# Second-layer sums of a dense network cut 16, 16 and 10 products long, beside an attention that shares TensorE

## Chip, cores and metric

The kernel runs on one core of one Trainium2 chip. The metric is device time in microseconds (us) of one execution, the median of several runs; less is better. The granted TensorE clock reads full speed through the whole profiled execution.

## What is computed

The input x has 2048 rows of 512. It is normalised by row, and the normalised rows go two ways: through an attention with 32 heads of width 16 that all share one key and one value projection, and through a dense network with 1792 hidden values. The result is x plus the product of the two.

```python
x = A_x
xn = _layernorm(x, axis=-1)
s = _A_ref(xn, A_wq, A_wk, A_wv, A_wo)          # attention
g = _silu(_B_ref(xn, B_w1, B_b1, B_w2))         # dense network
return x + s * g

def _A_ref(x, wq, wk, wv, wo):
    q = (x @ wq).reshape(B, S, H, Dh).transpose(0, 2, 1, 3)
    k = x @ wk
    v = x @ wv
    scores = jnp.einsum("bhqd,bkd->bhqk", q, k) * (Dh ** -0.5)
    p = _softmax(scores, axis=-1)
    o = jnp.einsum("bhqk,bkd->bhqd", p, v)
    return o.transpose(0, 2, 1, 3).reshape(B, S, H * Dh) @ wo

def _B_ref(x, w1, b1, w2):
    h = jnp.einsum("bsd,df->bsf", x, w1) + b1
    sp = jnp.log1p(jnp.exp(-jnp.abs(h))) + jnp.where(h > 0, h, 0)
    act = h * jnp.tanh(sp)                       # Mish
    return jnp.einsum("bsf,fd->bsd", act, w2)
```

## The kernel before

**Numbers.** Matrix products are made from float32 values split into a high and a low part. A product of two such values is three matmuls (`TERMS`, L56: high by high, high by low, low by high). Each of these is called a dense product below when it belongs to a projection or to the network.

**Attention in 512 steps.** The 2048 rows are cut into four chunks of 512 columns, and the work into 512 steps, sixteen for each of the 32 pairs of chunk and group of four heads. A step has

- four score products, `e` in the profile (L1056, function `score`), each over 64 rows of the array, then an exponent of each on ScalarE (ACT), `pts<-e` (L1061);
- four products for the largest score of a row, `m` (L1084, function `m_one`), also over 64 rows, each followed on VectorE (DVE) by a maximum, `mb<-m` (L1088). They run 22 steps ahead (`LEAD`);
- four value products, `pv` (L1142), over all 128 rows, from exponents made two steps earlier.

**Two halves of the array.** A 64-row product uses one half of TensorE's rows, and two of them, one on each half, run side by side. They are called a pair here. A dense product of 128 rows is split into its upper and its lower 64 rows (`Mm.half`, L114), and these dense halves, `xps` in the profile, fill the half of the array that the scores leave free. In one step the dense halves lie on one side and the scores on the other; in the next step the sides are exchanged.

**Buffers.** PSUM has three buffers for `e`, three for `m`, one for the dense sum and one for `pv`. The fourth `e` in a row therefore takes the buffer of the first one and needs its exponent done, and the fourth `m` needs the maximum of the first.

**Dense groups.** The dense work is a queue of groups, each a sum in one PSUM buffer: the query projections, the first layer (function `m1_group`), the output projections (`wo_groups`) with 12 products each, and the second layer. The second layer's 14 weight tiles give 42 products for each of 16 row tiles. They are cut into three parts (`THIRDS`, L53: tiles 0 to 4, 5 to 9, 10 to 13; function `m2_groups`), so 15, 15 and 12 products, whose sums are added by ACT and DVE outside PSUM.

**How a group is laid over steps.** There are two ways.

- Function `waves` (L610) lays a group of 12 over four steps of 6 halves: a step takes 6 dense products' halves on one side, the next step their other halves. With 6 halves one `m` goes to the dense side too, so that a step is seven pairs.
- Function `unit` (L672) lays a whole group over a block of four steps. A block has two halves; in each, the dense halves go through in a row on one side, while eight `e` and the `m` of two steps stand on the other, in the order of the string `UNIT` (L48). In it, E is a score product, M a max product, x stands for a place with a dense half alone, and 0 for a place with an `m` on the dense side and an `e` on the other. The last m takes a buffer of the scores. Behind the places stand two steps' `pv`. A block is used where a group of more than 12 and at most 15 products is ready at a step that four divides (`unit_ready`, L1541); a longer group that is not ready then goes through `waves`.

The Python code that writes the instructions decides all of this before the kernel runs. It keeps its own estimates of the time of a step (`K_US`, `UNIT_US`) to decide when transfers are issued and which group is ready.

**Weights.** Second-layer and output weights go through a ring of five tiles on the chip (`wbs`, L203); a group waits in the queue until its tiles are there. The query projection is copied by ACT into a tile `qf` (L741), split by GpSimd (POOL) into `qh` and `ql`, and moved by DMA into the query tiles `qt`. The attention's last step adds x, held in one of four tiles `xr`.

Of the kernel before, what the change touches and what calls it, by code (L numbers as in the profile page):

```python
# [41 lines left out]
STEP_US = 2.88  # L42
K_US = {-1: 2.3, 0: 2.7, 6: 2.86, 7: 3.07, 8: 3.07}
UNIT_US = 11.75
XMAX = 8
NPT = 14
EM = "MEMEMEME"
UNIT = "0MEMExEMEMEMEMEm"  # L48
MLAG = 4
NHB = 4  # L50
NACT = 10
AHEAD = 5
THIRDS = ((0, 5), (5, 10), (10, 14))  # L53
TMAX = 2.0 ** 14
EMAX = 2.0 ** 60
# [67 lines left out]
def block_kernel(ctx: ExitStack, tc: tile.TileContext, x, wq, wk, wv, wo, w1, b1, w2, out):  # L123
# [78 lines left out]
    b1c = cp.tile([P, NFT], F32, name="b1c")  # L202
    wbs = cp.tile([P, 5, 2, D], F32R, name="wbs")  # L203
    pts = cp.tile([P, NPT, C], F32, name="pts")
# [163 lines left out]
    def v_copy(c):  # L368
        vt_of[c] = sb.tile([P, C], F32, tag="xr", name=f"vt{c}", bufs=4)
# [26 lines left out]
    load_x(0)  # L396
    wkv = sb.tile([P, C], F32, tag="xr", name="wkv", bufs=4)
    wkv = wkv[:, 0:2 * NDT * DH].rearrange("p (a t n) -> p a t n", a=2, t=NDT)
# [41 lines left out]

    RING = {"wq": 1, "ws": 2, "wb": 5, "wx": 4}
    NRAW = {"wq": 1, "ws": 1, "wb": 1, "wx": 1}
# [23 lines left out]
    def home(tag, k):  # L466
        if tag == "wx":
            return (xt_of[NC] if k else new_xt(NC))[:, :, k]
        if tag == "ws" and k < 12 and k % 6 < 4:
            return xt_of["w"][:, :, k % 6]  # L470
        if tag == "wb":
            return wbs[:, (k - 1) % 5]
        return sb.tile([P, 2, D], F32R, tag=tag, name=f"{tag}{k}", bufs=RING[tag])

# [35 lines left out]
    def load(tag):  # L510
# [6 lines left out]
        it = its[n]  # L517
        if taken(tag, n) and (tag != "ws" or kept.get(it.key)):
            return
        if n == k and kept.get(it.key):  # L520
# [86 lines left out]
    def chunk_size(n):  # L607
        return -(-n // -(-n // XMAX)) if n else 0

    def waves(h, em, new):  # L610
# [44 lines left out]
        if k and not done:  # L655
# [5 lines left out]
            else:  # L661
                cur["chunk"] = mms

    def mm12(lhs, rhs, n, late=False):
        res = []
        tot = 3 * n
        for j, a, b in ([(j, a, b) for a, b in ((0, 0), (0, 1), (1, 0)) for j in range(n)] if late else
                        [(j, a, b) for j in range(n) for a, b in TERMS]):
            res.append(Mm(pe, lambda j=j, a=a: lhs(j, a), lambda j=j, b=b: rhs(j, b), len(res), tot))
        return res  # L670

    def unit(s, h):  # L672
# [24 lines left out]
        for n, op in enumerate(UNIT):  # L697
            if n == 8:
                due(t + 0.5)
                pump()  # L700
                due(t + 1)
            if op == "0":
                m_one(h)
                op = "E"
            elif xs:
                x_one()
# [23 lines left out]
    def q_group(c, b):  # L730
        it = item("wq", ("q", b), wq[:, P * b:P * (b + 1)].rearrange("(t p) n -> p t n", p=P))

        def post(ps):
# [3 lines left out]
            if first:  # L737
                act.activation(qh, ps, AF.Copy)
                lead["q"](lambda: sub(dve, ql, ps, f(qh)))
            else:  # L740
                qf = sb.tile([P, C], F32, tag="qf", name=f"qf{c}_{b}", bufs=1)  # L741
                act.activation(qf, ps, AF.Copy)
                gap[0] += 1
                hi_pool(qh, qf)
                sub(pool, ql, qf, f(qh))
            for k in range(2):
# [20 lines left out]
    t_hist = [-10 ** 6] * 2  # L767
    xr_hist = [-10 ** 6] * 4
    hb_hist = [-10 ** 6] * NHB
# [79 lines left out]

    def m2_groups(c, third, its, m1s):  # L850
        lo, hi = THIRDS[third]

        def ready(tt):
            done = m1_done.get((c, hi - 1))
            return None if done is None else done - g_of[tt].most
# [3 lines left out]
        def mk(tt):  # L859
            def post(ps):  # L860
# [36 lines left out]
                def s3():  # L897
# [22 lines left out]
    def wo_groups(c):  # L920
# [4 lines left out]
        def mk(tt):  # L925
# [79 lines left out]

    def w2_items(c, k):
        lo, hi = THIRDS[k]
        return [item(("wb", "wx")[(c, k) == (NC - 1, 2)], ("2", ft), w2[P * ft:P * (ft + 1), :]) for ft in range(lo, hi)]

# [9 lines left out]
    for c in range(NC):  # L1019
        for k in range(3):  # L1020
# [5 lines left out]
            take(THIRDS[k][1] - THIRDS[k][0] - 2)  # L1026
            g2 = m2_groups(c, k, w2_items(c, k), None)
            if (c, k) == (NC - 1, 1):
# [164 lines left out]
    def turn_rows():  # L1193
        t = sb.tile([P, C], F32, tag="qf", name="turns", bufs=1)
        for e in range(2):
# [345 lines left out]
    def unit_ready(s):  # L1541
# [151 lines left out]
```

## Time and profile before

| | |
|---|---|
| median of 3 runs | 1564.72 us (1564.71 to 1564.95) |
| span of the profiled execution | 1564.5 us; the profile gives no other time of it, and the median lies 0.2 us above |
| TensorE matmuls | 11715, busy 99% of the span |
| TensorE weight loads | 56% |
| VectorE | 86% |
| ScalarE | 83% |
| GpSimd | 41% |
| 16 DMA engines | 25%, 125 MB |
| attention steps with 6 dense halves | 362 |
| blocks of four steps | 31 |
| other steps with 8 or 7 dense halves | 2 and 2 |
| last steps, after the last max product | 22 |

The counts of steps and blocks are those of the program's order on TensorE. In the profile a line of a group has the engine, the operation, the tile written and those read, the count, the busy time, the mean time of one in ns, and the idle time of the engine before it with what ended it. In the time line a row has its start, its length (of several merged instructions: from the first start to the last end), the engine, the line of the code, the operation and its tiles. PEld is TensorE's load of weights, which can run beside a matmul.

A matmul's time in the time line overlaps with that of the next one on the same rows of the array. What counts is the distance from start to start.

### The profile page before, as it was taken

Reading aid. Unit: us, or ns where it says so; the run is one execution under the profiler, and the core shown is the slowest. Engines: PE = TensorE matmul, PEld = TensorE weight load, DVE = VectorE, ACT = ScalarE, POOL = GpSimd, SP = SyncE. Lnnn points to the kernel's source line nnn. Section 1 sums busy time; section 2 is a strip of 40 time slices with the busy share of each in tenths; the row PEclk is TensorE's granted clock in tenths of the full one; section 3 lists DMA queues with packets and bytes.
Section 4 is the critical chain, followed back from the end, with each engine's and each line's share of the span. In section 5 each row is a group of like instructions: output and inputs, shape, how many; then the busy total and the mean of one; then the engine's idle time right before and its main releaser. Section 6 shows DMA issues by size and latency. Waiting matters only on the chain.

```text
span 1564.5 us, 31399 instructions
## 1 busy us (share of the span) xinstructions
PE 1553.6 (99%) x11715; PEld 877.1 (56%) x11715; DVE 1347.6 (86%) x2279; ACT 1292.8 (83%) x2509; POOL 635.1 (41%) x667
## 2 busy tenths in 40 slices
PE   9999999999999999999999999999999999999998
PEld 6555655655555565565555556556555555655644
DVE  7998888888989988888898988888889998888844
ACT  6588888789888778977989787897788978888796
POOL 4787449365356203331615422163152323314122
PEclk9999999999999999999999999999999999999999
DMA  6333134133141303212113220322321213031110
GB/s 197 106 132 118 46 104 146 29 112 112 51 153 50 107 16 112 72 27 98 51 59 109 92 92 18 103 67 78 104 59 45 93 57 112 23 98 32 29 67 28
DMA packets 72083, 125.47 MB, mean 80 GB/s; under 512 B 19742, under 2 KB 33356, under 8 KB 71932
## 3 DMA queue, kind: packets, MB, share of 16 engines
q1 hardware_dynamic: 71500, 122.68, 24.8%
q8 instruction: 93, 1.52, 0.4%
q10 hardware_dynamic: 432, 0.79, 0.1%
q14 instruction: 58, 0.48, 0.1%
HBM read 75.57 MB, written 26.21 MB: 65 GB/s over the span
## 4 chain that ended last, share of the span: by engine, by line
PE 97%; DVE 2%; ACT 1%; POOL 0%; issue 0%; DVEq 0%
PE xps L116 43%; PE pv L1142 32%; PE m L1084 12%; PE e L1056 7%; DVE mb L1088 1%; PE xps L112 1%; PE warm L1310 1%; PE kp L350 0%; PE xp L309 0%; PE wop L116 0%; ACT pts L1061 0%; DVE e L888 0%; PE y2ps L116 0%; PE wop L112 0%; ACT hb L800 0%; ACT xt L318 0%
## 5 line engine op out<-in xcount | busy, mean ns | idle before, releaser
L1088 DVE TENSOR_REDUCE mb<-m 128x1 f32<-128x512 f32 x2048 | 1266.4, 683 | 167.5 <-PE m L1084 104.7
L1061 ACT ACTIVATE pts<-e 128x512 f32<-128x512 f32 x2048 | 1066.1, 607 | 219.9 <-PE e L1056 157.1
L1084 PE MATMUL m<-ks,qt 48*128 48x512 f32 (+1 forms) x2048 | 844.1, 425 | 1.3 <-DVE mb L1088 1.3
L1056 PE MATMUL e<-qt,ks 64*128 64x512 f32 x2048 | 748.8, 407 | 0.0
L1142 PE MATMUL pv<-pts,vaug 128*32 128x512 f32 x4096 | 532.9, 603 | 0.0
L1084 PEld LDWEIGHTS m<-ks,qt 48*128 48x128 f32 (+1 forms) x2048 | 369.9, 185 | 105.8 <-DVE mb L1088 50.8
L1056 PEld LDWEIGHTS e<-qt,ks 64*128 64x128 f32 x2048 | 373.5, 186 | 27.3 <-ACT pts L1061 22.8
L116 PE MATMUL xps<-wbs,act 64*128 64x512 f32 x1248 | 314.4, 397 | 0.0
L116 PE MATMUL xps<-xt,ws 64*128 64x512 f32 x1128 | 312.3, 410 | 1.7 <-ACT pts L1061 0.9
L116 PEld LDWEIGHTS xps<-xt,ws 64*128 64x128 f32 x1128 | 194.8, 185 | 185.6 <-ACT pts L1061 122.3
L116 PEld LDWEIGHTS xps<-wbs,act 64*128 64x128 f32 x1248 | 226.5, 185 | 64.8 <-ACT pts L1061 32.7
L1142 PEld LDWEIGHTS pv<-pts,vaug 128*32 128x32 f32 x4096 | 87.6, 108 | 150.6 <-issue 141.9
L169 POOL TENSOR_TENSOR hb<-hb,t 128x512 f32<-128x512 f32 x56 | 72.1, 1287 | 162.4 <-ACT t L819 82.1
L179 POOL TENSOR_SCALAR t<-t 128x512 f32<-128x512 f32 x56 | 34.4, 615 | 184.0 <-ACT t L806 183.9
L116 PE MATMUL xps<-xt,wq 64*128 64x512 f32 x336 | 93.0, 410 | 0.0
L116 PEld LDWEIGHTS xps<-xt,wq 64*128 64x128 f32 x336 | 58.0, 185 | 55.0 <-ACT pts L1061 37.7
L169 POOL TENSOR_TENSOR oc<-oc,sc 128x512 f32<-128x512 f32 (+1 forms) x16 | 20.6, 1289 | 153.4 <-DMA wbs<-w 71.2
L116 PE MATMUL xps<-wbs,ot_all 64*128 64x512 f32 x288 | 79.3, 408 | 0.0
L116 PEld LDWEIGHTS xps<-wbs,ot_all 64*128 64x128 f32 x288 | 49.6, 185 | 46.8 <-ACT pts L1061 28.5
L169 POOL TENSOR_TENSOR act<-hb,act 128x512 fp32r<-128x512 f32 x56 | 72.1, 1288 | 4.7
L169 POOL TENSOR_TENSOR hb<-hb,u 128x512 f32<-128x512 f32 x56 | 72.1, 1288 | 4.4
L169 POOL TENSOR_TENSOR u<-u,t 128x512 f32<-128x512 f32 x56 | 72.0, 1285 | 4.7
(160 smaller groups left out, 885.5 us busy)
## 6 DMA issues: line engine op xcount, KB each, us to landing
wbs<-w SPq DMA_DIRECT2D x38, 512.0 KB
ws<-w SPq DMA_DIRECT2D x36, 512.0 KB
qt<-qh SPq DMA_DIRECT2D x256, 32.0 KB
w<-wbs SPq DMA_DIRECT2D x14, 512.0 KB
wq<-wq SPq DMA_DIRECT2D x14, 512.0 KB
wbs<-wo SPq DMA_DIRECT2D x12, 512.0 KB
rawws<-in_dram SPq DMA_DIRECT2D x20, 256.0 KB
w<-ws SPq DMA_DIRECT2D x10, 512.0 KB
```

Source lines behind the costliest of these rows:

```text
L112: self.pe.matmul(ps, self.lhs(), self.rhs(), start=(self.k == 0), stop=(self.k == self.tot - 1))
L116: i = self.pe.matmul(ps, self.lhs()[o], self.rhs()[o], start=(self.k == 0 and self.halves == 0), stop=(self.k == self.tot - 1 and self.hal ...
L169: eng.tensor_tensor(out=o, in0=a, in1=b, op=op)
L179: pool.tensor_scalar(o, o, lim, 0.0, op0=ALU.min, op1=ALU.max)
L1056: pe.matmul(e, ks[o:o + 64, P * k:P * (k + 1)], q[o:o + 64, p], start=True, stop=True)
L1061: x = act.activation(dst, e, AF.Exp, scale=0.25)
L1084: pe.matmul(m, q[o, p, P * t:P * (t + 1)], ks[o, C * kb:C * (kb + 1)], start=True, stop=True)
L1088: return dve.reduce_max(out=mb_of[v][:, kb, z:z + 1], in_=m, axis=AX.X)
L1142: pe.matmul(o[32 * j:32 * j + 32], vaug[:, k], pt, start=(k == 0), stop=(k == 15))
L1310: pe.matmul(warm, qts[0][:, 0, 0:P], qts[0][:, 0], start=True, stop=True)
```

## The change

The second layer's 42 products of a row tile stand in one list, weight tile by weight tile, and are cut at 16 and 32: parts of 16, 16 and 10 products for 15, 15 and 12. A cut can now fall within a weight tile, so tiles 5 and 10 are used by two parts. The items for weights are made once for each chunk and tile (`w2_item`), not once for each part.

The string `UNIT` becomes sixteen places that all have a dense half on one side and an `e` or an `m` on the other: the `m` that stood beside the first `e` moves to the place that had a dense half alone. Blocks take groups of up to 16.

A group of 10 is laid over two steps of 6 and two of 4 halves (`chunk_size` rounds up to an even number).

The ring of second-layer weights gets a sixth tile. Room for it comes from `qf`, which goes (ACT copies into `ql` itself, and POOL subtracts in place), and from the fourth `xr` tile; the last row tile's x goes to an `hb` tile. Two of the planner's estimates, for steps with 0 and with 4 halves, are new.

```diff
-K_US = {-1: 2.3, 0: 2.7, 6: 2.86, 7: 3.07, 8: 3.07}
+K_US = {-1: 2.3, 0: 2.65, 4: 2.68, 6: 2.86, 7: 3.07, 8: 3.07}
-UNIT = "0MEMExEMEMEMEMEm"
+UNIT = "EMEMEMEMEMEMEMEm"
+CUTS = (0, 16, 32, 42)
+NWB = 6
...
-    wbs = cp.tile([P, 5, 2, D], F32R, name="wbs")
+    wbs = cp.tile([P, NWB, 2, D], F32R, name="wbs")
...
-    RING = {"wq": 1, "ws": 2, "wb": 5, "wx": 4}
+    RING = {"wq": 1, "ws": 2, "wb": NWB, "wx": 4}
...
+        if tag == "wb" and n == NWB - 1 and todo["ws"][0] < 10:
+            return
...
     def chunk_size(n):
-        return -(-n // -(-n // XMAX)) if n else 0
+        m = -(-n // -(-n // XMAX)) if n else 0
+        return m + m % 2
...
+    def mm_list(lhs, rhs, terms):
+        return [Mm(pe, lambda j=j, a=a: lhs(j, a), lambda j=j, b=b: rhs(j, b), n, len(terms))
+                for n, (j, a, b) in enumerate(terms)]
...
     def unit(s, h):
-            if op == "0":
-                m_one(h)
-                op = "E"
-            elif xs:
+            if xs:
                 x_one()
...
-                qf = sb.tile([P, C], F32, tag="qf", name=f"qf{c}_{b}", bufs=1)
-                act.activation(qf, ps, AF.Copy)
+                act.activation(f(ql), ps, AF.Copy)
                 gap[0] += 1
-                hi_pool(qh, qf)
-                sub(pool, ql, qf, f(qh))
+                hi_pool(qh, f(ql))
+                sub(pool, ql, f(ql), f(qh))
...
-    xr_hist = [-10 ** 6] * 4
+    xr_hist = [-10 ** 6] * 3
...
-    def m2_groups(c, third, its, m1s):
+    w2_terms = [(j, a, b) for j in range(NFT) for a, b in TERMS]
+
+    def m2_groups(c, third):
         lo, hi = THIRDS[third]
+        terms = w2_terms[CUTS[third]:CUTS[third + 1]]
+        fts = sorted({j for j, a, b in terms})
+        its = [w2_item(c, j) for j in fts]
...
-            g = Group(mm12(lambda j, a: act_of[c, lo + j][:, a, P * tt:P * (tt + 1)],
-                           lambda j, b: its[j].tile[:, b], hi - lo), post, its, [lambda: ready(tt)])
+            g = Group(mm_list(lambda j, a: act_of[c, j][:, a, P * tt:P * (tt + 1)],
+                              lambda j, b: w2_of[c, j].tile[:, b], terms), post, its, [lambda: ready(tt)])
...
-            g.late = 3 if hi - lo == 5 else 2
+            g.late = len(its) - 2
...
-                if xr_hist[-4] is None:
-                    return False
-                st["x"] = sb.tile([P, D], F32, tag="xr", name=f"xr{t}", bufs=4)
-                st["free"] = hold(xr_hist)
+                if last and tt == 3:
+                    st["x"] = sb.tile([P, D], F32, tag="hb", name=f"xr{t}", bufs=NHB)
+                    st["free"] = lambda: None
+                else:
+                    if xr_hist[-3] is None:
+                        return False
+                    st["x"] = sb.tile([P, D], F32, tag="xr", name=f"xr{t}", bufs=3)
+                    st["free"] = hold(xr_hist)
...
-        return ok and 12 < len(cur["g"].mms) <= len(UNIT) - 1
+        return ok and 12 < len(cur["g"].mms) <= len(UNIT)
```

Two places on TensorE carry the prediction. In the rows `e_k_p_a` is a score product on side a (0 or 1), `m_a_n` a max product on side a, `xps` a dense half. The change adds lines above, so its line numbers are 2 to 14 higher. The first place is the start of the first half of the block at step 68, before and with the change; the dense halves are on side 0.

```order
1216 L1084 MATMUL m_0_20_3867<-ks,qt_79 128x512
1217 L1056 MATMUL e_4_0_1_3870<-qt_78,ks 128x512
1218 L116 MATMUL xps<-wbs,act_5_1624 128x512
1219 L1084 MATMUL m_1_20_3874<-ks,qt_79 128x512
1220 L116 MATMUL xps<-wbs,act_5_1624 128x512
1221 L1056 MATMUL e_4_1_1_3878<-qt_78,ks 128x512
1222 L116 MATMUL xps<-wbs,act_5_1624 128x512
1223 L1084 MATMUL m_1_21_3882<-ks,qt_79 128x512
1224 L116 MATMUL xps<-wbs,act_6_1718 128x512
1225 L1056 MATMUL e_5_0_1_3886<-qt_78,ks 128x512
1226 L116 MATMUL xps<-wbs,act_6_1718 128x512 x2
1227 L1056 MATMUL e_5_1_1_3891<-qt_78,ks 128x512
```

The same place with the change:

```order
1236 L118 MATMUL xps<-wbs,act_5_1625 128x512
1237 L1070 MATMUL e_4_0_1_3881<-qt_78,ks 128x512
1238 L118 MATMUL xps<-wbs,act_5_1625 128x512
1239 L1098 MATMUL m_1_20_3885<-ks,qt_79 128x512
1240 L118 MATMUL xps<-wbs,act_6_1716 128x512
1241 L1070 MATMUL e_4_1_1_3889<-qt_78,ks 128x512
1242 L118 MATMUL xps<-wbs,act_6_1716 128x512
1243 L1098 MATMUL m_1_21_3893<-ks,qt_79 128x512
1244 L118 MATMUL xps<-wbs,act_6_1716 128x512
1245 L1070 MATMUL e_5_0_1_3897<-qt_78,ks 128x512
1246 L118 MATMUL xps<-wbs,act_7_1935 128x512
1247 L1098 MATMUL m_1_22_3901<-ks,qt_79 128x512
```

The half's first max product stood in the first place, on the dense side (row 1216); now its first is in the second place, on the side of the scores (row 1239), and a dense half stands in the first. Where two dense halves came in a row (row 1226) a max product now stands between them (row 1247). All eight `m` of a half are on the side of the scores.

The second place is step 102, the third step of a group of the third part, before and with the change, up to the value products (of the repeated dense halves some rows are left out).

```order
1685 L116 MATMUL xps<-wbs,act_12_3675 128x512
1686 L1084 MATMUL m_1_24_5263<-ks,qt_78 128x512
1687 L116 MATMUL xps<-wbs,act_12_3675 128x512
1688 L1056 MATMUL e_6_0_1_5267<-qt_77,ks 128x512
1690 L1084 MATMUL m_1_25_5271<-ks,qt_78 128x512
1692 L1056 MATMUL e_6_1_1_5275<-qt_77,ks 128x512
1694 L1084 MATMUL m_1_26_5279<-ks,qt_78 128x512
1696 L1056 MATMUL e_7_0_1_5283<-qt_77,ks 128x512
1697 L1084 MATMUL m_0_24_5286<-ks,qt_78 128x512
1698 L1056 MATMUL e_7_1_1_5289<-qt_77,ks 128x512
```

The same place with the change:

```order
1718 L1098 MATMUL m_1_24_5281<-ks,qt_78 128x512
1719 L118 MATMUL xps<-wbs,act_13_3864 128x512
1720 L1070 MATMUL e_6_0_1_5285<-qt_77,ks 128x512
1721 L118 MATMUL xps<-wbs,act_13_3864 128x512
1722 L1098 MATMUL m_1_25_5289<-ks,qt_78 128x512
1723 L118 MATMUL xps<-wbs,act_13_3864 128x512
1724 L1070 MATMUL e_6_1_1_5293<-qt_77,ks 128x512
1725 L1098 MATMUL m_0_24_5296<-ks,qt_78 128x512
1726 L1070 MATMUL e_7_0_1_5299<-qt_77,ks 128x512
1727 L1098 MATMUL m_0_25_5302<-ks,qt_78 128x512
1728 L1070 MATMUL e_7_1_1_5305<-qt_77,ks 128x512
```

Seven pairs became six: two dense halves are gone, and a second `m` went to the dense side. The first score stays in the second pair, and the fourth score moves from the seventh pair to the sixth.

The order of the dense groups, the 140 steps at which one begins, the number of blocks (31) and the order of ACT's instructions are the same before and with the change. Of the steps with 6 halves, 26 become steps with 4. One second-layer group that goes through `waves`, at steps 160 to 163, had 8, 8, 7 and 7 halves and has 8 in each step. Three third parts lie in the last 22 steps.

More of the change, by code (lines that the diff above doesn't have):

```diff
@@ L368, in v_copy @@
     def v_copy(c):
-        vt_of[c] = sb.tile([P, C], F32, tag="xr", name=f"vt{c}", bufs=4)
+        vt_of[c] = sb.tile([P, C], F32, tag="xr", name=f"vt{c}", bufs=3)
         if c == 0:
@@ L396, in block_kernel @@
     load_x(0)
-    wkv = sb.tile([P, C], F32, tag="xr", name="wkv", bufs=4)
+    wkv = sb.tile([P, C], F32, tag="xr", name="wkv", bufs=3)
     wkv = wkv[:, 0:2 * NDT * DH].rearrange("p (a t n) -> p a t n", a=2, t=NDT)
@@ L471, in home @@
         if tag == "wb":
-            return wbs[:, (k - 1) % 5]
+            return wbs[:, (k - 1) % NWB]
         return sb.tile([P, 2, D], F32R, tag=tag, name=f"{tag}{k}", bufs=RING[tag])
@@ L662, in waves @@
                 cur["chunk"] = mms
+    def mm_list(lhs, rhs, terms):
+        return [Mm(pe, lambda j=j, a=a: lhs(j, a), lambda j=j, b=b: rhs(j, b), n, len(terms))
+                for n, (j, a, b) in enumerate(terms)]
     def mm12(lhs, rhs, n, late=False):
[L665 to L670, printed above, removed]
+        return mm_list(lhs, rhs, [(j, a, b) for a, b in TERMS for j in range(n)] if late else
+                       [(j, a, b) for j in range(n) for a, b in TERMS])
     def unit(s, h):
@@ L848, in m1_group @@
         return g
-    def m2_groups(c, third, its, m1s):
+    w2_terms = [(j, a, b) for j in range(NFT) for a, b in TERMS]
+    def m2_groups(c, third):
         lo, hi = THIRDS[third]
+        terms = w2_terms[CUTS[third]:CUTS[third + 1]]
+        fts = sorted({j for j, a, b in terms})
+        its = [w2_item(c, j) for j in fts]
         def ready(tt):
-            done = m1_done.get((c, hi - 1))
+            done = m1_done.get((c, fts[-1]))
             return None if done is None else done - g_of[tt].most
@@ L1004, in xt_loads, with w2_item @@
         g.start = lambda: (old(), loads())
-    def w2_items(c, k):
-        lo, hi = THIRDS[k]
-        return [item(("wb", "wx")[(c, k) == (NC - 1, 2)], ("2", ft), w2[P * ft:P * (ft + 1), :]) for ft in range(lo, hi)]
+    w2_of = {}
+    def w2_item(c, ft):
+        if (c, ft) not in w2_of:
+            tag = "wx" if c == NC - 1 and ft > THIRDS[2][0] else "wb"
+            w2_of[c, ft] = item(tag, ("2", ft), w2[P * ft:P * (ft + 1), :])
+        return w2_of[c, ft]
     qqueue.extend(q_group(c, b) for c in range(NC) for b in range(4))
@@ L1026, in block_kernel @@
             take(THIRDS[k][1] - THIRDS[k][0] - 2)
-            g2 = m2_groups(c, k, w2_items(c, k), None)
+            g2 = m2_groups(c, k)
             if (c, k) == (NC - 1, 1):
@@ L1193, in turn_rows @@
     def turn_rows():
-        t = sb.tile([P, C], F32, tag="qf", name="turns", bufs=1)
+        t = sb.tile([P, C], F32, tag="ql", name="turns", bufs=1)
         for e in range(2):
```

## Prediction, made before the change was run

> **What bounds the kernel now.** I read the page first: the shares of the engines and the chain that ended last.
>
> ```profile
> PE 1553.6 (99%) x11715; PEld 877.1 (56%) x11715; DVE 1347.6 (86%) x2279; ACT 1292.8 (83%) x2509; POOL 635.1 (41%) x667
> PE 97%; DVE 2%; ACT 1%; POOL 0%; issue 0%; DVEq 0%
> ```
>
> TensorE is busy 99% of the span and the chain runs through it for 97%. That reads as "fewer products, less time". But a matmul that was let in late is busy too, so the share doesn't say whether the array streams or waits. The time line of single steps does. Next I read busy times by stretch: the block shown below, the sum over all 31, then 80 steps of 6 halves in a row.
>
> ```profile
> 184.03:195.91 11.88, 11.88 (x98) 7.74 (x94) 9.62 (x17) 10.00 (x19) 5.11 (x5) 1.00 0.23 59
> ...
> sum 372.09, PE 372.09 PEld 238.72 DVE 320.93 ACT 296.52 POOL 110.82; mean PE 12.00 PEld 7.70 DVE 10.35 ACT 9.57 POOL 3.57
> 312.68:541.38 228.70, 228.70 (x1764) 123.57 (x1756) 205.88 (x349) 197.54 (x380) 115.79 (x117) 1.00 0.30 94
> ```
>
> A block takes 12.00 us on average, 11.88 where nothing disturbs it; a step of 6 halves takes 228.70 / 80 = 2.86. The change touches the 31 blocks and 26 of the steps. So two questions decide: what ends a block's half, and what ends a step.
>
> **A block's half.** This is the time line from 184.03 on, the first half of the block at step 36. The rows are its two first max products, the maxima, the exponents, and the end.
>
> ```profile
> 185.00 0.50 PE L1084 MATMUL m<-ks,qt 48*128 48x512 f32 x1
> 185.34 0.40 PE L116 MATMUL xps<-wbs,act 64*128 64x512 f32 x1
> 185.34 0.39 PE L1084 MATMUL m<-ks,qt 48*128 48x512 f32 x1
> 185.53 4.28 DVE L1088 TENSOR_REDUCE mb<-m 128x1 f32<-128x512 f32 x7 [1.20 <-PE e L1056]
> 185.56 3.04 ACT L1061 ACTIVATE pts<-e 128x512 f32<-128x512 f32 x6 [0.25 <-PE e L1056]
> ...
> 188.07 0.18 PEld L1084 LDWEIGHTS m<-ks,qt 48*128 48x128 f32 x1
> 188.07 0.50 PE L1084 MATMUL m<-ks,qt 48*128 48x512 f32 x1
> ...
> 188.41 0.39 PE L1056 MATMUL e<-qt,ks 64*128 64x512 f32 x1
> 188.59 0.39 PE L116 MATMUL xps<-wbs,act 64*128 64x512 f32 x1
> 188.66 0.18 PEld L1084 LDWEIGHTS m<-ks,qt 48*128 48x128 f32 x1
> 188.66 0.50 PE L1084 MATMUL m<-ks,qt 48*128 48x512 f32 x1
> 189.09 0.64 PE L1142 MATMUL pv<-pts,vaug 128*32 128x512 f32 x4
> ```
>
> The dense halves run from 185.34 to 188.59 in fourteen distances, 0.23 us each: that is the time of a pair. The maxima run without a pause from 0.03 us after the first m has ended. Seven take 4.28 us, so they follow each other in (4.28 - 0.68) / 6 = 0.60 us, slower than the max products come, one in two pairs or 0.46 us. The seventh m needs the fourth maximum's buffer. That maximum ends at 185.53 + 3 x 0.60 + 0.68 = 188.01, and the m's weight load and matmul both start at 188.07. **It was waiting for DVE.** It lasts 0.50 us instead of 0.39, because its weights weren't in the array before, and the next e on its side comes 0.34 us later, not 0.24.
>
> The eighth m stands in a buffer of the scores and waits for the sixth exponent, which ends at 185.56 + 3.04 = 188.60; it starts at 188.66, again with its load, and the value products come 0.43 us later. So a half ends by two chains, DVE's and ACT's, that here end almost together. The array's pairs don't bound it.
>
> With the change, the first m stands where the second stood: it ends at 185.34 + 0.39 = 185.73 instead of 185.50, and the maxima start at 185.76. The fourth ends 0.23 us later too, at 188.24, so the seventh m starts at 188.30. The e behind it comes 0.34 later, at 188.64, the eighth m 0.24 later, at 188.88. The sixth exponent is done by then (188.60, as before): its score stands in the eleventh place, 185.34 + 9 x 0.23 = 187.41, ends 0.4 later, and has its turn on ACT at 188.60 - 0.64 = 187.96. So this m has its weights in time, and value products follow a matmul of that kind by 0.34 us (198.41 to 198.75 in the fence on the step, below): 189.22 for 189.09. **The half loses 0.13 us**, although dense products fill one more place in it. Queued behind the waiting m on TensorE are that e, the last m, two dense halves with time to spare on their own side, and the value products of two steps; the next half and the exponents of the last scores wait for those.
>
> Of the 62 halves, 42 have this shape in the time line to within 0.03 us, which costs 42 x 0.13 = 5.5 us. Eight are the first halves behind a block whose sum DVE adds up. Here the addition has pushed the last maximum back:
>
> ```profile
> 289.08 0.68 DVE L1088 TENSOR_REDUCE mb<-m 128x1 f32<-128x512 f32 x1
> 289.70 0.50 PE L1084 MATMUL m<-ks,qt 48*128 48x512 f32 x1
> 289.82 0.50 PE L1056 MATMUL e<-qt,ks 64*128 64x512 f32 x1
> ...
> 293.88 1.92 PE L1142 MATMUL pv<-pts,vaug 128*32 128x512 f32 x16
> ```
>
> The first e waits for that maximum (289.08 + 0.68 + 0.05), 0.12 us. With the change it waits another 0.10, since the maxima of the half ahead run 0.23 us late and its end only 0.13. The first m now stands behind that e, 0.22 us late, where before it stood ahead of it and on time. From first m to value products such a half took 293.88 - 289.70 = 4.18 us, the common one 189.09 - 185.00 = 4.09. Counted from the same point it takes 4.09 + 0.13 + 0.22 = 4.44 now: 0.26 us more, eight times, 2.1 us. In nine halves another ACT instruction delays the exponents:
>
> ```profile
> 178.92 0.50 PE L1084 MATMUL m<-ks,qt 48*128 48x512 f32 x1
> 179.60 3.07 ACT L1061 ACTIVATE pts<-e 128x512 f32<-128x512 f32 x6
> ...
> 183.14 1.50 PE L1142 MATMUL pv<-pts,vaug 128*32 128x512 f32 x12
> ```
>
> They take 183.14 - 178.92 = 4.22, already 0.13 us more by ACT's chain, and DVE's now fits beneath: no loss. In three more it is 0.5 us more: none either. The blocks' sum is **+7.6 us**.
>
> The bounds of this term: if a late m's weights hid, the e would follow by 0.24 and the end be 189.12, +0.03 in each of 50 halves, or 1.5 us. If the eighth m were also let in late, the end would be 188.88 + 0.43 = 189.31, +0.22 in each, or 11 us. I take the value that the rows of the late m show.
>
> The Trainium skill, "TensorE: Matmul & The Clock Gate", section "Step-by-step: what each phase is for", says that weight loads are pulled ahead of matmuls in flight while the matmuls stay in order. By that rule the late m would cost its wait alone, the +1.5 us. The trace shows its load starting with the matmul at 188.07, so the rule doesn't reach a load that itself waits.
>
> **A step of 4 halves.** No step before has four. This is one of six, from 195.91 to 198.75: the first e, the exponents, the sixth pair's dense half, the fourth e and the end.
>
> ```profile
> 197.23 0.40 PE L1056 MATMUL e<-qt,ks 64*128 64x512 f32 x1
> 197.68 2.07 ACT L1061 ACTIVATE pts<-e 128x512 f32<-128x512 f32 x4 [0.49 <-PE e L1056]
> 198.15 0.39 PE L116 MATMUL xps<-xt,ws 64*128 64x512 f32 x1
> 198.33 0.18 PEld L1056 LDWEIGHTS e<-qt,ks 64*128 64x128 f32 x1
> 198.41 0.42 PE L1056 MATMUL e<-qt,ks 64*128 64x512 f32 x1
> 198.75 1.07 PE L1142 MATMUL pv<-pts,vaug 128*32 128x512 f32 x8
> ```
>
> One pair less looks like 0.23 us less. But the fourth e needs the buffer of the first, whose exponent ends at 197.68 + 0.60 = 198.28 (the mean of L1061 on the page is 607 ns), and its weight load starts at 198.33, just behind. With 4 halves the first e stands where it stood, in the second pair; the fourth moves from the seventh pair to the sixth, whose turn is at 198.15, and finds its buffer closed until 198.33. What an e costs that is let in late is shown by a step in which ACT was late:
>
> ```profile
> 1157.90 2.08 ACT L1061 ACTIVATE pts<-e 128x512 f32<-128x512 f32 x4
> 1158.58 0.18 PEld L1056 LDWEIGHTS e<-qt,ks 64*128 64x128 f32 x1 [0.21 <-ACT pts L1061]
> 1158.58 0.49 PE L1056 MATMUL e<-qt,ks 64*128 64x512 f32 x1
> 1159.00 1.07 PE L1142 MATMUL pv<-pts,vaug 128*32 128x512 f32 x8
> ```
>
> Load and matmul start together and the end is 0.42 us behind. So the step of 4 ends at 198.33 + 0.42 = 198.75, where it ended before. **I take 0 for the 26 steps**; bounds: -0.23 each (-6.0 us) if the pair counted, +0.05 each (+1.3 us) if exponents start no earlier than in the latest ordinary steps. DVE isn't the limit there: four maxima are 4 x 0.60 = 2.40 us.
>
> The Trainium skill, "TensorEngine Tiling (Array Packing)", section "PSUM Bottleneck", warns that tiling the array speeds up TensorE but not the emptying of PSUM. That rule speaks against this change, and the rows agree with it: both places wait for a buffer to be emptied.
>
> **The rest.** One group goes from 8, 8, 7, 7 halves to 8 in each. The last 22 steps lose six dense products, on steps that don't get shorter with fewer:
>
> ```profile
> 541.38:544.44 3.06, 3.06 (x26) 1.70 (x24) 2.69 (x6) 2.74 (x7) 1.91 (x2) 1.00 0.91 307
> 550.57:553.62 3.05, 3.05 (x25) 1.64 (x24) 2.47 (x5) 2.05 (x5) 0.00 (x0) 1.00 0.24 53
> 1504.41:1527.84 23.43, 23.43 (x183) 10.21 (x181) 8.59 (x5) 22.09 (x45) 5.17 (x5) 1.00 0.13 35
> 1542.37:1547.07 4.70, 4.70 (x33) 2.02 (x31) 0.00 (x0) 4.12 (x9) 0.00 (x0) 1.00 0.02 3
> ```
>
> Steps of 8 and of 7 halves take 3.06 and 3.05; ten last steps with six halves take 2.34 each, two with three take 2.35. I cost both edits at 0. ACT now writes a query group into `ql` itself and so has to wait for the DMAs that read the last one:
>
> ```profile
> 242.23 0.59 SPq L756 DMA_DIRECT2D qt<-ql  x1
> 252.88 0.60 ACT L742 ACTIVATE qf<-xps 128x512 f32<-128x512 f32 x1
> ```
>
> At the closest they are issued 10.6 us ahead: 0. If it did wait, the exponents behind it on ACT, and by the chains above TensorE, would wait as long. The sixth weight tile moves a few loads on SP and splits on POOL earlier, past transfers of query rows. TensorE's wait list names no DMA ahead of it, and groups begin at the same steps: 0, with 1 us either way.
>
> **Sum.** 1564.5 + 7.6 = 1572.1 by the profiled execution's span. The median of the runs lies 0.2 above it: **1572.3 us**.
>
> **Rivals.** (a) *The pair counts.* If the late e in the step of 4 streamed at once and the maxima made up their 0.23 us, each step would save 0.23: 1564.7 - 6.0 = 1558.7, faster. It decides at one point: the first exponent would have to end before 198.15. The row at 198.33 speaks against it; the 99% speak for it. Chance 0.14. (b) *The late m costs its wait alone.* By the bound of 1.5 us this gives 1566.2. The row at 188.07 speaks against it. 0.10. The rule on weight loads of the Trainium skill's page "TensorE: Matmul & The Clock Gate" would have it so. (c) *Both terms, nearly cancelling*: the blocks lose 7.6 and the steps save 6.0, 1566.3. 0.09. (d) *Late maxima pile up* into the steps behind a block, or both m come late: 11 us and more, 1576 to 1582. DVE's 10.35 us of 12.00 leave room, which speaks against it. 0.07. (e) *The blocks aren't used*, sixteen products running as four steps of 8, 4 x 3.06 = 12.24 for 12.00: +7.4. The order has 31 blocks still, so it gets no chance of its own.
>
> **How the numbers follow.** My forecast, blocks slower and steps the same, has 0.60, with 1567.5 to 1577 as its own range. The range of 1564 to 1579 leaves out (a) and the top of (d), near 0.19. What a measurement can tell from no change is about 0.2%, 3 us. Faster by more than that: (a), 0.14. Within: (b) and (c), 0.19. Slower: the rest, 0.67.
>
> **What would show it.** In the time line after: a clean block of 12.15 us for 11.88; the seventh m of a half starting with its load 0.23 us later than before, and the end 0.8 to 0.95 us behind it; steps of 4 halves with the fourth e's load and matmul starting together, 2.85 long. Steps of 2.62 would prove (a) right in that part, and an e 0.24 us behind the late m would prove (b).

## The result, and the profile after

| kernel | median | runs | ratio to before |
|---|---|---|---|
| before | 1564.82 us | 1564.71 to 1564.95 | |
| changed | 1574.17 us | 1573.45 to 1577.32 | 1.0059 (1.0044 to 1.0074) |

The change makes the kernel slower by 9.35 us at the median; 7.6 were forecast. The profiled execution is the longest of the four (1577.32 us, span 1575.5): TensorE's clock was lower in its lead, which the last experiment separates. The first rows of the page of the changed kernel, engines and chain:

```profile
PE 1564.9 (99%) x11715; PEld 852.6 (54%) x11715; DVE 1348.9 (86%) x2279; ACT 1293.1 (82%) x2509; POOL 635.2 (40%) x667
...
PE 98%; DVE 1%; ACT 0%; DMA 0%; issue 0%
```

They look as before. The same number of matmuls takes 11 us more on a TensorE that is again "99% busy"; 2.0 us of that lie ahead of the first value product (at 89.08 us for 87.07). Busy times by stretch (start and end, length, then the busy times of PE, PEld, DVE, ACT, POOL, the granted clock, the DMA share and GB/s) show the block at step 36, then the sums of the 31 blocks, of the 26 steps of 4 halves, and of the 13 six-half steps that follow a group's last step of 4:

```profile
186.46:198.57 12.11, 12.11 (x101) 7.14 (x97) 9.74 (x17) 10.00 (x19) 5.09 (x5) 1.00 0.23 58
...
sum 380.29, PE 380.29 PEld 220.06 DVE 319.27 ACT 296.57 POOL 111.19; mean PE 12.27 PEld 7.10 DVE 10.30 ACT 9.57 POOL 3.59
...
sum 74.10, PE 74.10 PEld 34.93 DVE 64.96 ACT 65.31 POOL 27.24; mean PE 2.85 PEld 1.34 DVE 2.50 ACT 2.51 POOL 1.05
...
sum 38.30, PE 38.30 PEld 19.12 DVE 38.30 ACT 31.96 POOL 14.27; mean PE 2.95 PEld 1.47 DVE 2.95 ACT 2.46 POOL 1.10
```

Before, the blocks took 372.09: they lost **8.2 us**. The steps of 4 take 2.85 each, and a step of 6 took 2.86: the same 26 steps took 74.08 us before, so the 52 dense halves that left them, a pair in each step, saved nothing. The 13 steps took this before:

```profile
sum 37.41, PE 37.41 PEld 19.12 DVE 37.41 ACT 30.98 POOL 14.17; mean PE 2.88 PEld 1.47 DVE 2.88 ACT 2.38 POOL 1.09
```

So another **0.9 us** went there. The two make 9.1 of the 9.35.

**A half of a block.** The time line of the changed kernel, first half of the block at step 36:

```profile
187.44 0.50 PE L1070 MATMUL e<-qt,ks 64*128 64x512 f32 x1
...
187.77 0.39 PE L1098 MATMUL m<-ks,qt 48*128 48x512 f32 x1
...
188.00 3.04 ACT L1075 ACTIVATE pts<-e 128x512 f32<-128x512 f32 x6 [0.25 <-PE e L1070]
...
188.20 4.88 DVE L1102 TENSOR_REDUCE mb<-m 128x1 f32<-128x512 f32 x8 [1.20 <-PE m L1098]
...
190.15 0.49 PE L1098 MATMUL m<-ks,qt 48*128 48x512 f32 x1
...
190.74 0.18 PEld L1098 LDWEIGHTS m<-ks,qt 48*128 48x128 f32 x1 [0.22 <-DVE mb L1102]
190.75 0.50 PE L1098 MATMUL m<-ks,qt 48*128 48x512 f32 x1
...
190.85 0.19 PEld L1070 LDWEIGHTS e<-qt,ks 64*128 64x128 f32 x1
...
191.08 0.39 PE L1070 MATMUL e<-qt,ks 64*128 64x512 f32 x1
...
191.09 0.18 PEld L1098 LDWEIGHTS m<-ks,qt 48*128 48x128 f32 x1
191.32 0.39 PE L1098 MATMUL m<-ks,qt 48*128 48x512 f32 x1
...
191.63 1.92 PE L1156 MATMUL pv<-pts,vaug 128*32 128x512 f32 x16
```

The first m starts one pair behind the first e, the maxima start behind it at 188.20, and the fourth ends at 188.20 + 3 x 0.60 + 0.68 = 190.68. The seventh m starts at 190.74 with its load; the next e follows 0.33 us later, the eighth m 0.24 after that with its load ahead, the value products 0.31 after that. The sixth m (190.15) is let in late too, 0.07 behind the third maximum (188.20 + 1.20 + 0.68 = 190.08). From the half's first products to the value products it is 4.19 us, 4.09 before.

**A step of 4 halves.** Step 102 of the changed kernel, its maxima, exponents, last pair and end:

```profile
380.91 1.89 DVE L1102 TENSOR_REDUCE mb<-m 128x1 f32<-128x512 f32 x3 [0.37 <-PE m L1098]
...
381.12 2.06 ACT L1075 ACTIVATE pts<-e 128x512 f32<-128x512 f32 x4 [0.27 <-PE e L1070]
...
381.40 0.39 PE L1070 MATMUL e<-qt,ks 64*128 64x512 f32 x1
...
381.66 0.18 PEld L1098 LDWEIGHTS m<-ks,qt 48*128 48x128 f32 x1 [0.31 <-DVE mb L1102]
...
381.77 0.18 PEld L1070 LDWEIGHTS e<-qt,ks 64*128 64x128 f32 x1
381.77 0.49 PE L1070 MATMUL e<-qt,ks 64*128 64x512 f32 x1
...
382.19 0.64 PE L1156 MATMUL pv<-pts,vaug 128*32 128x512 f32 x4
```

The first exponent ends about 0.60 after 381.12; the fourth e's load and matmul start together 0.05 later, 0.37 behind the third e for a pair's 0.23, and the end is 0.42 behind. The fourth m, in the same pair, waited for the first maximum and was let in only 0.11 earlier: a second chain stands close behind the first.

### The profile page after: what moved, and what is told of

The parts are those of the page before. It is cut to its first block, busy times and chain, and to the rows that moved or that the text cites. A ratio compares the mean times of both kernels' runs of the same rounds, so it can differ in the third digit from the quotient of the medians.

```text
span 1575.5 us, 31421 instructions
## 1 busy us (share of the span) xinstructions
PE 1564.9 (99%) x11715; PEld 852.6 (54%) x11715; DVE 1348.9 (86%) x2279; ACT 1293.1 (82%) x2509; POOL 635.2 (40%) x667
## 4 chain that ended last, share of the span: by engine, by line
PE 98%; DVE 1%; ACT 0%; DMA 0%; issue 0%
PE xps L118 43%; PE pv L1156 32%; PE m L1098 12%; PE e L1070 7%; PE xps L114 1%; DVE mb L1102 1%; PE kp L352 1%; PE warm L1324 1%; PE wop L118 0%; PE xp L311 0%; PE wop L114 0%; PE y2ps L118 0%; DMA ks<-ks 0%; ACT pts L1075 0%; ACT hb L801 0%; ACT xt L320 0%
## 5 line engine op out<-in xcount | busy, mean ns | idle before, releaser
L1070 PE MATMUL e<-qt,ks 64*128 64x512 f32 x2048 | 757.3, 406 | 0.0
L118 PE MATMUL xps<-wbs,act 64*128 64x512 f32 x1270 | 333.8, 406 | 0.0
L118 PEld LDWEIGHTS xps<-wbs,act 64*128 64x128 f32 x1270 | 218.3, 184 | 118.0 <-ACT pts L1075 45.3
```

The costliest lines, as they stand in the source:

```text
L118: i = self.pe.matmul(ps, self.lhs()[o], self.rhs()[o], start=(self.k == 0 and self.halves == 0), stop=(self.k == self.tot - 1 and self.hal ...
L1070: pe.matmul(e, ks[o:o + 64, P * k:P * (k + 1)], q[o:o + 64, p], start=True, stop=True)
```

## The experiments

Each kernel is the changed one with the edit shown. Ratios are to the kernel before, run on the same chip (medians 1564.80 to 1565.42).

| run | edit | median us | ratio (95%) | 31 blocks us |
|---|---|---|---|---|
| e1_rest_only | old places, old cuts | 1565.06 | 1.0001 (0.9992 to 1.0010) | 372.15 |
| e2_order_only | new places, old cuts | 1572.95 | 1.0042 (1.0030 to 1.0055) | 379.40 |
| e3_m_early | last m's earlier | 1566.36 | 1.0002 (0.9993 to 1.0011) | 371.39 |
| e7_m_early_15 | the same, old cuts | 1564.57 | 0.9997 (0.9988 to 1.0007) | 371.47 |
| e8_max_first | M before E | 1578.70 | 1.0084 (1.0069 to 1.0099) | 384.80 |
| e4_score_first | steps of 4 | 1572.50 | 1.0037 (1.0025 to 1.0050) | 380.18 |
| e5_four_first | 4, 4, 6, 6 | 1573.38 | 1.0055 (1.0041 to 1.0069) | 380.28 |
| e6_both | e3, e4 and e5 | 1561.58 | 0.9978 (0.9969 to 0.9987) | 371.43 |
| e9_changed_again | none | 1575.18 | 1.0063 (1.0051 to 1.0076) | 380.35 |

### Which part of the change costs

```diff
# e1_rest_only
-UNIT = "EMEMEMEMEMEMEMEm"
+UNIT = "0MEMExEMEMEMEMEm"
-CUTS = (0, 16, 32, 42)
+CUTS = (0, 15, 30, 42)
-            if xs:
+            if op == "0":
+                m_one(h)
+                op = "E"
+            elif xs:
                 x_one()
...
# e2_order_only
-CUTS = (0, 16, 32, 42)
+CUTS = (0, 15, 30, 42)
-            if xs:
+            if xs and (n or len(g.mms) == 16):
                 x_one()
```

> The change without its two main parts: cuts at 15 and 30 and the old order of a block's places, as before; the six weight tiles, the query copy into ql, three xr tiles and the planner's new numbers stay. Theory (the time is lost in the order of a block's places, on the chain from max products to DVE's maxima and back): the rest costs nothing, 1564.8 us as before, within 1 us; a clean half 5.06 from value products to value products. Rival (weights, splits and copies that run earlier or wait longer cost part of the 9.4 us): 1567 to 1574.

> The new order of a block's places with sums of 15, 15 and 12 products: all eight max products of a half on the side of the scores, the first one behind the first score, but fifteen dense halves (none in the half's first place). Theory (the first max product stands one pair later, so DVE's maxima run one pair later): a clean half 5.17 to 5.20 for 5.06, the held halves 5.40, blocks +8 us; the steps of 4 halves are gone, so the extra wait behind them too: 1572 to 1573.5 us. Rival (the sixteenth dense half fills the array's last free place, and that is what costs): no loss, 1565 us.

Both came out as the theory had it. Without the new places and cuts nothing is lost (1.0001), so the sixth weight tile, the query copy and the rest cost nothing. With the new places alone, at 15 dense halves, the blocks take 379.40 us, all but 0.9 of what they take with 16, and the 13 steps are back at 37.40. The blocks of e2, by stretch:

```profile
sum 379.40, PE 377.56 PEld 195.31 DVE 319.15 ACT 296.63 POOL 112.21; mean PE 12.18 PEld 6.30 DVE 10.30 ACT 9.57 POOL 3.62
```

So 7.3 of the 8.2 us come without the sixteenth dense half: it is **the first max product's place** that costs.

### What a half ends by

```diff
# e3_m_early (e7_m_early_15: also CUTS = (0, 15, 30, 42))
-UNIT = "EMEMEMEMEMEMEMEm"
+UNIT = "EMEMEMEMEMEMEmME"
-            if xs:
-                x_one()
+            for i in range(2 if n == 14 else 1):
+                if xs:
+                    x_one()
...
# e8_max_first
-UNIT = "EMEMEMEMEMEMEMEm"
+UNIT = "MEMEMEMEMEMEMEEm"
```

> The changed kernel, its sixteen dense halves kept, with the end of a half in another order: the max product in a buffer of the scores goes from the sixteenth place to the fourteenth (it then waits for the fifth exponent, not the sixth), the eighth max product from the fourteenth to the fifteenth, where the fourth maximum is done when its turn comes, and the last score from the fifteenth to the sixteenth, where it waits for the sixth exponent. The last dense half moves ahead of the fifteenth place's max product. The first score of the next half no longer takes the buffer of the last max product. Theory: no max product is let in late, a half ends by ACT's chain: clean and held halves 5.00 to 5.08 for 5.17 and 5.40, blocks -7 to -9 us against the changed kernel: 1565 to 1567 us. Rival (sixteen dense halves cost a pair each, 62 x 0.12): stays at 1573 to 1575 us.

> The new end of a block's half with sums of 15, 15 and 12 products, so one dense half less in each half of a block. Theory (a half ends by ACT's chain, and the sixteenth dense half lies beside it): clean halves 5.03 to 5.08, as with sixteen; blocks 371 us, 1564.5 us. Rival (the dense halves bound the half once the max products are not late): 0.1 to 0.23 less in each half, blocks 358 to 366 us, 1553 to 1560 us.

> The changed kernel with the order of a block's first fourteen places turned round, a max product ahead of each score: M first, then E, up to the place ahead of the last score. DVE's maxima then start one pair earlier, and ACT's exponents one pair later. Theory (a half ends by two chains, DVE's and ACT's, that end almost together, so one pair given to one is taken from the other): the last max product, in a buffer of the scores, waits for the sixth exponent, which now ends 0.23 us later: clean halves 5.20 to 5.30, no better than 5.17, 1574 to 1579 us. Rival (DVE's chain alone bounds a half): clean halves go back to 5.06 or less, 1564 to 1567 us.

In e3 the loss of the blocks is gone with all sixteen dense halves kept: 371.39 for 380.29. The time line of e3, the end of the first half at step 36, with the start of its exponents and maxima:

```profile
184.45 3.04 ACT L1076 ACTIVATE pts<-e 128x512 f32<-128x512 f32 x6 [0.25 <-PE e L1071]
...
184.66 3.68 DVE L1103 TENSOR_REDUCE mb<-m 128x1 f32<-128x512 f32 x6 [1.20 <-PE m L1099]
...
186.60 0.18 PEld L1099 LDWEIGHTS m<-ks,qt 48*128 48x128 f32 x1
186.60 0.50 PE L1099 MATMUL m<-ks,qt 48*128 48x512 f32 x1
...
186.94 0.39 PE L1071 MATMUL e<-qt,ks 64*128 64x512 f32 x1
...
187.41 0.39 PE L1099 MATMUL m<-ks,qt 48*128 48x512 f32 x1
...
187.55 0.18 PEld L1071 LDWEIGHTS e<-qt,ks 64*128 64x128 f32 x1
187.64 0.41 PE L1071 MATMUL e<-qt,ks 64*128 64x512 f32 x1
...
187.98 0.64 PE L1157 MATMUL pv<-pts,vaug 128*32 128x512 f32 x4
```

The fourth maximum ends at 184.66 + 1.80 + 0.68 = 187.14, and its m starts at 187.41, in its turn. But the theory wasn't right in one thing: the sixth m (186.60, with its load) is still let in late, 0.06 behind the third maximum (184.66 + 1.20 + 0.68 = 186.54). From there the products on its side follow without a further wait, at 186.94, 187.17, 187.41 and 187.64, and the value products 0.34 behind the last. The last e's load starts 0.06 behind the sixth exponent (184.45 + 3.04 = 187.49). Had its turn come earlier, this e would have started with its load at 187.55, and with the 0.42 of a late e the value products would come at 187.97, where they come now. So DVE's chain and ACT's end this half together, 4.09 us behind its first e (183.89); the theory named ACT's alone. The clean halves take 5.03 to 5.11 us from value products to value products, the ones behind an addition too. With one dense half less (e7) the blocks take 371.47, the same. The rival, that dense halves bound a half, falls from both sides.

In e8 DVE starts earlier and the half is longer. Its first half at step 36:

```profile
185.77 0.50 PE L1098 MATMUL m<-ks,qt 48*128 48x512 f32 x1
...
186.34 4.28 DVE L1102 TENSOR_REDUCE mb<-m 128x1 f32<-128x512 f32 x7 [1.35 <-PE m L1098]
...
186.57 3.08 ACT L1075 ACTIVATE pts<-e 128x512 f32<-128x512 f32 x6 [0.48 <-PE e L1070]
...
189.69 0.18 PEld L1098 LDWEIGHTS m<-ks,qt 48*128 48x128 f32 x1 [0.29 <-ACT pts L1075]
189.70 0.50 PE L1098 MATMUL m<-ks,qt 48*128 48x512 f32 x1
...
190.12 0.64 PE L1156 MATMUL pv<-pts,vaug 128*32 128x512 f32 x4
```

The maxima start 0.57 us behind the half's first pair (0.77 in the changed kernel), the exponents 0.80 (0.57 there). The last m waits for the sixth exponent, 186.57 + 3.08 = 189.65, and the half takes 190.12 - 185.77 = 4.35. The clean halves take 5.29 to 5.36 us, at the top of the 5.20 to 5.30 expected or a little above. One pair given to one chain was taken from the other: **two chains bound a half**, and which one is late is a matter of the order.

### The steps of 4 halves, and the step behind them

```diff
# e4_score_first (a constant, then in waves, then where the steps are laid)
+EM4 = "EMEMEMEM"
...
+        ahead = k == 4
         while a or b or xs:
-            if xs:
+            if ahead:
+                ahead = False
+                b.popleft()()
+            elif xs:
...
-                for op in EM:
+                for op in EM4 if k == 4 else EM:
...
# e5_four_first, in chunk_size
+        if n == 10:
+            return 4
         m = -(-n // -(-n // XMAX)) if n else 0
```

> The changed kernel, with the 26 steps of 4 dense halves in another order: they begin with a score beside a max product, and the dense halves start one pair later; so the first exponent can start one pair earlier. Theory (a step of 4 halves ends when the fourth score gets the first one's buffer, whose exponent is done 0.23 us after that score's turn): with the first exponent a pair earlier the step ends a pair earlier, 2.62 for 2.85, 26 x 0.23 = 6.0 us less than the changed kernel: 1568 us. Rival (the step is bound by DVE's four maxima at 0.60 us each, 2.4 us and what follows behind it, or by ACT's four exponents with other ACT work): stays at 2.80 or more, 1573 to 1574 us.

> The changed kernel, with the groups of 10 laid 4, 4, 6, 6 for 6, 6, 4, 4, so that the addition of the finished sum on DVE falls into a step behind one of 6 halves. Theory (the addition stands ahead of maxima when it follows a step of 4, and the fourth max product of the next step is let in late): the thirteen six-half steps behind such a group go back from 2.93 to 2.97 to about 2.88, 0.6 to 0.9 us in all, to be read from the trace since the runs can't tell so little: 1573.3 us. Rival (these steps are late from the six weight tiles' transfers or from a query copy, not from the addition): they stay at 2.93 to 2.97.

In e4 the 26 steps take 2.71 each. The sum of the 26 by stretch, then the time line of step 102:

```profile
sum 70.36, PE 70.36 PEld 31.72 DVE 63.40 ACT 65.87 POOL 26.04; mean PE 2.71 PEld 1.22 DVE 2.44 ACT 2.53 POOL 1.00
```

```profile
378.20 1.89 DVE L1107 TENSOR_REDUCE mb<-m 128x1 f32<-128x512 f32 x3 [0.33 <-PE e L1075]
378.24 1.57 ACT L1080 ACTIVATE pts<-e 128x512 f32<-128x512 f32 x3
...
378.95 0.18 PEld L1103 LDWEIGHTS m<-ks,qt 48*128 48x128 f32 x1 [0.28 <-DVE mb L1107]
378.95 0.49 PE L1103 MATMUL m<-ks,qt 48*128 48x512 f32 x1
...
378.95 0.49 PE L1075 MATMUL e<-qt,ks 64*128 64x512 f32 x1
...
379.38 0.64 PE L1161 MATMUL pv<-pts,vaug 128*32 128x512 f32 x4
```

The exponents start early enough now, and the gain is 0.145 us a step for the 0.23 expected, because the chain close behind takes over: the fourth m waits for the first maximum (378.20 + 0.68), starts with its load at 378.95 and ends the step with a late m's 0.43 instead of 0.34. The mechanism was right, the size expected 1.6 times too large, and the new end, DVE's maxima, is what the rival had named. The 26 steps gained 3.7 us, but the 13 steps behind them lost 0.5 more (38.83 in all); why stays open. The median, 1572.50, lies between the 1568 expected and the rival's 1573 to 1574.

In e5 the 13 steps take 37.39 us, as before the change. Eight of them have 4 halves there, which by itself shortens nothing, as the 26 show; the other five have 6 and take 2.87 or 2.88 us each, for 2.94 to 2.97 in the changed kernel. In e2, which has the change's blocks and its weight tiles but no steps of 4, the 13 take 37.40 with 6. The addition is what delayed them. DVE's time line in the changed kernel around the start of step 104 (385.04), and in the kernel before around the same start (381.19):

```profile
383.75 0.69 DVE L1102 TENSOR_REDUCE mb<-m 128x1 f32<-128x512 f32 x1 [0.36 <-PE m L1098]
384.43 0.69 DVE L875 TENSOR_TENSOR y<-xps,y 128x512 f32<-128x512 f32 x1
385.04 3.67 DVE L1102 TENSOR_REDUCE mb<-m 128x1 f32<-128x512 f32 x6
```

```profile
379.91 1.29 DVE L1088 TENSOR_REDUCE mb<-m 128x1 f32<-128x512 f32 x2 [0.37 <-PE m L1084]
381.11 0.68 DVE L869 TENSOR_TENSOR y<-xps,y 128x512 f32<-128x512 f32 x1
381.71 1.28 DVE L1088 TENSOR_REDUCE mb<-m 128x1 f32<-128x512 f32 x2
```

With 4 halves the sum is done earlier in the step, so the addition stands ahead of three of its maxima, not two. Six then run without a pause; the fourth of them, step 104's first, ends at 385.04 + 1.80 + 0.68 = 387.52, and step 104's fourth m is let in behind it.

### The three edits together

> The changed kernel with all three edits: the end of a block's half as in the run with the early max product, steps of 4 halves that begin with a score, and 4, 4, 6, 6. Theory (three places, each with its own wait, which add up): blocks 371.4 us, steps of 4 halves 2.71, so 1565.1 - 26 x 0.145 - 0.7 = 1560.6 us, 0.25 to 0.3% faster than the kernel before. Rival (the time that one place gives up comes back in the next one, since DVE then runs late): 1564 to 1566 us.

1561.58 us, **faster than both kernels**: 0.22% under the one before (0.13 to 0.31%). The gains of e3 and e4 add up; that of e5 hardly comes on top of e4's, and there the rival was right in part. The 58 steps of the third parts (13 groups of four steps) and right behind them take 167.9 us in the changed kernel, 167.0 in e5, 164.7 in e4 and 164.4 in e6: 3.5 us less, where 4.5 were expected, which is the 1.0 us that is missing. In e6 eight steps of 4 follow an addition and take 2.88 each, not 2.71.

### The changed kernel again

> The changed kernel unaltered, for a second profile and a narrower interval. Theory (the lower granted clock before the first value product in its first profile is not of the change): blocks 380.2 us and steps of 4 halves 2.85 as in the first profile, the time up to the first value product back to 86 to 87 us for 89.1, the median 1573 to 1574.5 us. Rival (the change makes the clock drop there): 89 us again in the profiled execution and in most others.

The blocks (380.35 us) and the 26 steps (74.06) repeat to 0.1 us; the first value product starts at 85.56 us, for 89.08 in the first profile and 86 to 87 expected. The median is 0.7 above the expected range, as the runs lie at 1573.8 and at 1576.9 us with one between. A window of 11 us in the lead, before the first value product, in the first profile of the changed kernel, in the second, and in the profile before (the clock is the third number from the end):

```profile
24.00:35.00 11.00, 10.99 (x41) 5.65 (x42) 6.53 (x12) 8.98 (x26) 3.22 (x6) 0.53 0.41 137
```

```profile
24.00:35.00 11.00, 10.51 (x58) 5.84 (x57) 9.68 (x17) 10.93 (x33) 4.02 (x6) 1.00 0.42 140
```

```profile
24.00:35.00 11.00, 10.98 (x52) 6.15 (x51) 8.82 (x16) 10.17 (x30) 3.68 (x8) 0.84 0.42 137
```

The first profile of the changed kernel had the clock at 0.53 there, the second at full, and before had 0.84: it differs between two runs of one kernel, so the change doesn't set it. The spans of the changed kernel are 1575.5 and 1571.9.

## Why the prediction was right, and where it was off

The predicted 1572.3 us, slower, came from the right mechanism; 1.9 us were missing. Of these 0.9 lie in 13 steps behind the steps of 4, 0.6 in three halves, and 0.1 in the base, as the kernel before ran at 1564.82 beside the changed one, not 1564.7. About 0.3 are in no stretch looked at.

- **Clean half, +0.13 forecast.** Measured +0.127 in 39 halves, 5.0 us. The steps of the working hold one by one: m late by DVE with its load, next e 0.33 behind (0.34 forecast), eighth m in its turn (0.24), value products 0.31 behind (0.34). In the bounds the value taken was right; the "wait alone" (+0.03, rival b) isn't what happened: the late m's own load starts with it. The working missed that the sixth m is let in late as well; here that costs nothing of its own, since the seventh waits longer, but in e3 it is part of what ends the half. What the Trainium skill, "TensorE: Matmul & The Clock Gate", section "Step-by-step: what each phase is for", says of loads pulled ahead does show one instruction later: the e's load at 190.85 runs beside the late m.
- **Eight held halves, +0.26.** Measured +0.27, 2.2 us. Right.
- **Mis-sized: 42 halves counted as clean.** Three of them (the first halves at steps 68, 212 and 340) went from 5.06 to 5.39 to 5.41, +0.34 each for 0.13: they too begin with an e that waits for a late maximum, which before was done in time (277.06 + 0.68 = 277.74, the e at 277.81). The time line of the changed kernel at step 68:

```profile
279.94 0.68 DVE L1102 TENSOR_REDUCE mb<-m 128x1 f32<-128x512 f32 x1
280.67 0.18 PEld L1070 LDWEIGHTS e<-qt,ks 64*128 64x128 f32 x1
```

  The load starts 0.05 behind the maximum (280.62). The term measured 1.0 us for the 0.4 counted. In e3, where that buffer goes to another product, the three are back at 5.03 to 5.05.
- **Twelve halves bound by ACT's other work, 0.** Measured 0.03 us in all.
- **26 steps of 4 halves, 0.** Measured 0, with load and matmul of the fourth e together, as forecast. "DVE isn't the limit there" was true by 0.11 us only; e4 met it at once.
- **The rest, 0: the step that failed.** Copy, weights, ring and tail do cost nothing (e1). But 13 six-half steps lost 0.9 us because the addition moved ahead of a maximum, and the working never placed it; e5 shows it. Only the pile-up rival spoke of late maxima in steps behind.
- **The base, 1564.5 + 0.2.** The sum is the measured median, so it holds, but its parts hide two things that cancel in it: runs of both kernels list times 1.8 us above their spans (1564.79 beside 1563.0), and the profiled execution of before was slowed by its clock of 0.84, so that it was longer than a common run by 1.5 us. That the clock reads full speed through the whole profiled execution, as the first section says, isn't so: it does from the first value product on, not in the lead.

Rival (a) had the 99% for it and was wrong: the pair counts only when nothing else lets the next product in. Its condition, an earlier first exponent, is what e4 made, and then the steps did get shorter, by 0.145 us and not by the whole 0.23 of a pair.

## What to carry over

A TensorE that is 99% busy can still be paced by the engines that empty its buffers; the sign is a weight load that starts together with its matmul, and the engine to look at is the one whose row ends 0.05 to 0.07 us before. In a rotation of buffers, work out for each product which earlier one frees its buffer and when, and put the products that need late buffers last; in e3 the sixteen dense halves then fitted beside them at no cost. Starting one chain earlier gains nothing where it delays another that ends as late, as e8 shows. When an addition to a slow engine moves in the order, place it among that engine's other work before costing it at nothing.

## What the hardware showed beside that

The clock granted to TensorE in the lead differs from run to run of the same kernel. Over the 11 us shown it was 0.53 and full in the two profiles of the changed kernel, and 0.84 in the one before; in the first it read 0.50 in every microsecond from 25 to 34. The lost clock is (1 - 0.53) x 11 = 5.2 us there and (1 - 0.84) x 11 = 1.8 in the profile before; at half speed these are stretches of 10.4 and 3.5 us. By the Trainium skill, "TensorE: Matmul & The Clock Gate", section "What's actually happening", the clock goes to half and back by the activity seen in windows of 3.4 us. Three such windows and one have these lengths, so the trace agrees in that; that activity decides it, no run here shows. In time the loss is smaller than in clock: the first value product of the changed kernel starts 3.5 us later in the slower lead (89.08 for 85.56), more than a third of the effect studied here.

A product that is let in late costs more than its wait: 0.50 us for 0.39, with the next one on its side 0.33 or 0.34 us later for 0.23 or 0.24.
